# Scale and add in three stretches: the stretches' sizes on a grid of 128 bytes instead of 1 KiB

## The chip, the cores and the metric

One core of a Trainium2 chip. The metric is the device time of one execution in microseconds, the median of several runs. Before the change it is 150.83 us (three runs, 150.75 to 150.89).

## The reference

Two large arrays are read, one is scaled by a single number, and they are added:

```python
B, S, D = 512, 32, 640
x:  (B, S, D) bfloat16
fx: (B, S, D) bfloat16
alpha: (1,) bfloat16

def reference(x, fx, alpha):
    return x + alpha * fx
```

Each array has 10,485,760 elements of 2 bytes, 20.97 MB. Two are read and one is written: 62.9 MB.

## The kernel before

The arrays are taken as one flat row of elements. That row is cut into three stretches by `CUTS`, counted in units of `K` elements a partition: 63, 61 and 36 units of 512 elements (1 KiB). A stretch is a block of consecutive memory, shared out over the 128 partitions of the on-chip memory: partition p has the p-th part of it. In the first stretch each partition's row is 63 KiB long, and the rows of neighbouring partitions begin 63 KiB apart in memory; in the second it is 61, in the third 36.

All data lie in one on-chip tile, `room`, of `ROOM` = 207 units a partition. The arrays do not fit at once, so places in it are used again: a stretch of fx is loaded, scaled in place, added onto x, and its place is free for the next load. A second tile, `kept`, lies in the matmul accumulators' memory (PSUM) and takes 14 units of scaled fx out of `room`, so that a place comes free earlier.

The order is written out by hand in `PLAN`, a line for each step, and `tile_standalone__rezero__sampling_kernel` goes through it:

- `f a b @ t` and `x a b @ t` load the units a to b of fx or x to unit t of `room` (function `transfer`, line 109, all on SyncE's queue).
- `a` loads alpha (line 98), spreads it over the partitions with a matmul by ones (line 103) and copies it to `a_f` (line 104).
- `m t n` scales n units at t by alpha (line 122, VectorE).
- `p t n` copies n scaled units to `kept` (line 127), `q t n` adds `kept` to n units of x (line 139).
- `+ t u n` adds n scaled units at u to n units of x at t (line 144).
- `s a b @ t` stores (line 109); the first store has the words `after + 184`, by which it also waits for the addition at unit 184 (`late`, line 94).

SyncE issues in the order of the plan, and each issue waits until its place in `room` is free, or its data are there. Every issue goes to one queue, which 16 DMA engines work off in order. Each transfer covers all 128 partitions, eight rows for each engine. There are eleven data transfers: the first f load in two parts, the first x load, the second f load, the second x load in two parts, the third f and x loads, three stores.

The rows that a transfer touches are made here:

Of the kernel before, what the change touches and what calls it, by code (L numbers as in the profile page):

```python
# [1 line left out]

# [4 lines left out]

ALU = mybir.AluOpType
F32 = mybir.dt.float32
I32 = mybir.dt.int32  # L10

K = 512
P = 128
ROOM = 207
CUTS = (0, 63, 124, 160)
KEPT = 14

PLAN = """  # L30
f 0 8 @ 144
f 8 63 @ 152
a
x 0 63 @ 0
m 144 63
f 63 124 @ 63
+ 0 144 38
x 63 99 @ 146
+ 38 182 25
x 99 124 @ 182  # L40
m 63 61
p 110 14
f 124 160 @ 110
+ 146 63 36
x 124 160 @ 63
+ 182 99 2
m 110 36
+ 184 101 9
s 0 63 @ 0 after + 184
q 193 14  # L50
s 63 124 @ 146
+ 63 110 36
s 124 160 @ 63
"""


@with_exitstack
def kernel(
    ctx: ExitStack,
    tc: tile.TileContext,  # L60
    x: bass.AP,
    fx: bass.AP,
    alpha: bass.AP,
    out: bass.AP,
):
    nc = tc.nc
    flat = {
        name: t.rearrange("b s d -> (b s d)") for name, t in (("x", x), ("f", fx), ("s", out))
    }
    assert flat["x"].shape[0] == P * CUTS[-1] * K  # L70

    def stretch(what, a, b):
        low, high = next(c for c in zip(CUTS, CUTS[1:]) if c[0] <= a < c[1])
        rows = flat[what][P * low * K : P * high * K].rearrange("(p n) -> p n", p=P)
        return units(rows, a - low, b - low)

    consts = ctx.enter_context(tc.tile_pool(name="consts", bufs=1))
    psum = ctx.enter_context(tc.tile_pool(name="psum", bufs=1, space=bass.MemoryType.PSUM))
    rooms = ctx.enter_context(tc.tile_pool(name="rooms", bufs=1))
    ctx.enter_context(tc.manual_schedule())  # L80

    kept = psum.tile([P, KEPT * K], x.dtype, name="kept")
    room = rooms.tile([P, ROOM * K], x.dtype, name="room")
    a_f = consts.tile([P, 1], F32, name="a_f")
    info = mybir.DependencyInfo(mybir.DependencyClass.Sync, mybir.DependencyReason.DATA)
    done, moved = [], {}

    def units(t, a, b):
        return t[:, a * K : b * K]

    def late(r, after):
        if after:
            what, a = after[1], int(after[2])
            tc.add_manual_dep(r.ins, moved[what, a].ins.name, info, reason="issued late")

    def spread_alpha(after):
        a_1 = consts.tile([1, 1], alpha.dtype, name="a_1")
        done.append(nc.sync.dma_start(out=a_1[:], in_=alpha[None, :]))  # L98
        late(done[-1], after)
        ones = consts.tile([1, P], alpha.dtype, name="ones")  # L100
        nc.vector.memset(ones[:], 1.0)  # L101
        a_ps = psum.tile([P, 1], F32, name="a_ps")
        done.append(nc.tensor.matmul(a_ps[:], ones[:], a_1[:], start=True, stop=True))  # L103
        nc.vector.tensor_copy(out=a_f[:], in_=a_ps[:])  # L104

    def transfer(what, a, b, at, after):
        away, here = stretch(what, a, b), units(room, at, at + b - a)
        out, in_ = (away, here) if what == "s" else (here, away)
        r = nc.sync.dma_start(out=out, in_=in_)  # L109
        late(r, after)  # L110
        moved[what, a] = r
        done.append(r)

    for step in PLAN.strip().split("\n"):
        what, *rest = step.split()
        if what == "a":
            spread_alpha(rest)
        elif what == "m":
            t, n = map(int, rest)
            f = units(room, t, t + n)  # L120
            done.append(
                nc.vector.tensor_scalar(out=f, in0=f, scalar1=a_f[:], scalar2=None, op0=ALU.mult)  # L122
            )
        elif what == "p":
            t, n = map(int, rest)
            done.append(
                nc.vector.tensor_scalar(  # L127
                    out=units(kept, 0, n).bitcast(I32),
                    in0=units(room, t, t + n).bitcast(I32),
                    scalar1=0,  # L130
                    scalar2=None,
                    op0=ALU.bitwise_or,
                )
            )
        elif what == "q":
            t, n = map(int, rest)
            xt = units(room, t, t + n)
            done.append(
                nc.vector.tensor_tensor(out=xt, in0=xt, in1=units(kept, 0, n), op=ALU.add)  # L139
            )  # L140
        elif what == "+":
            t, u, n = map(int, rest)
            xt, f = units(room, t, t + n), units(room, u, u + n)
            moved[what, t] = nc.vector.tensor_tensor(out=xt, in0=xt, in1=f, op=ALU.add)  # L144
            done.append(moved[what, t])
        else:
            a, b, _, at = rest[:4]
            transfer(what, int(a), int(b), int(at), rest[4:])

    last = nc.sync.nop(nofuse=True)  # L150
    for i in done[:-1]:
        tc.add_manual_dep(last.ins, i.ins.name, info, reason="all but the last store")


# [1 line left out]
_INS = ['x', 'fx', 'alpha']  # L156
_OUTS = [((512, 32, 640), 'bfloat16')]


# [23 lines left out]
```

## Time and profile before

| | |
|---|---|
| median of three runs | 150.83 us |
| the profiled execution's own time | 150.75 us |
| its span, first to last instruction | 149.0 us |
| VectorE busy | 69.4 us, 13 instructions |
| DMA queue | 62.92 MB, 422 GB/s over the span |
| read, written | 41.94 MB, 20.97 MB |
| VectorE idle before the first addition, until the first x load | 10.4 us |
| VectorE idle before two scalings, until the second and third f load | 1.4 and 7.0 us |

The span lies inside the device time; 1.75 us of this execution are outside of it. The profile also records every packet that the DMA engines move, with its size, its start and its duration. For data a packet is one partition's row of one transfer, so that each of the 16 engines has 8 packets a transfer and 88 in all.

### The profile page before, as it was taken

The numbers are of one execution on the slowest core, as the hardware profiler recorded it, in microseconds if no ns is written. First come the engines' busy times: TensorE is split into PE (matmuls) and PEld (weight loads), VectorE is DVE, ScalarE is ACT, GpSimd is POOL, SyncE is SP. The second block draws the span as 40 slices with busy tenths as digits, with TensorE's granted clock in tenths as the row PEclk, the third lists the DMA queues.
The fourth block names the chain that finished last, engine by engine and source line by source line (L and its number), as shares of the span: only waits on it lengthen the run. The fifth ranks groups of instructions, "written<-read, shape, count | busy, mean of one in ns | idle before, by whom it ended". The sixth has DMA issues, their size and how long they took to land.

```text
span 149.0 us, 80 instructions
## 1 busy us (share of the span) xinstructions
PE 0.2 (0%) x1; PEld 0.1 (0%) x1; DVE 69.4 (47%) x13; POOL 0.2 (0%) x4
## 2 busy tenths in 40 slices
PE   0000000000000000000000000000000000000000
PEld 0000000000000000000000000000000000000000
DVE  0000009920099996999999009999950000000000
POOL 0000000000000000000000000000000000000000
DMA  5996998996969969989999989999696998969993
GB/s 176 590 439 287 484 519 364 468 537 294 546 268 537 520 285 427 475 376 422 419 454 475 445 346 475 475 436 554 277 554 277 546 419 386 537 268 427 475 475 158
DMA packets 1586, 62.92 MB, mean 422 GB/s; under 512 B 178, under 2 KB 178, under 8 KB 178
## 3 DMA queue, kind: packets, MB, share of 16 engines
q1 hardware_dynamic: 1586, 62.92, 98.0%
HBM read 41.94 MB, written 20.97 MB: 422 GB/s over the span
## 4 chain that ended last, share of the span: by engine, by line
DMA 38%; DVE 27%; DVEq 7%; another core or an unknown queue 1%; SPq 1%; issue 0%
DMA room<-in_x_dram 26%; DVE room L144 13%; DMA room<-in_fx_dram 11%; DVE room L122 9%; DVEq L178 7%; DVE kept L127 3%; DVE room L139 2%; SPq L109 1%; SPq L98 0%; DVEq L122 0%; DVEq L144 0%
## 5 line engine op out<-in xcount | busy, mean ns | idle before, releaser
L144 DVE TENSOR_TENSOR room<-room 128x18432 bf16<-128x18432 bf16 (+4 forms) x6 | 39.7, 6641 | 10.4 <-DMA room<-in_x_dram 10.4
L122 DVE TENSOR_SCALAR room<-room,a_f 128x32256 bf16<-128x32256 bf16 (+2 forms) x3 | 22.0, 7331 | 8.4 <-DMA room<-in_fx_dram 8.3
L104 DVE COPY a_f<-a_ps 128x1 f32<-128x1 f32 x1 | 0.2, 157 | 21.1 <-PE a_ps L103 21.1
L127 DVE TENSOR_SCALAR kept<-room 128x3584 int32<-128x3584 int32 x1 | 3.9, 3894 | 0.0
L139 DVE TENSOR_TENSOR room<-room,kept 128x7168 bf16<-128x7168 bf16 x1 | 3.9, 3881 | 0.0
L101 DVE MEMSET ones<- 1x128 bf16 x1 | 0.2, 165 | 0.8 <-PEq L167 0.8
L103 PE MATMUL a_ps<-a,ones 1*128 1x1 bf16 x1 | 0.2, 158 | 21.9 <-DMA a<-in_alpha_dram 21.9
L167 POOL MEMSET const-uint8-127<- 128x1 uint8 x1 | 0.1, 102 | 0.0
L167 POOL MEMSET const-bfloat16-1.0<- 128x1 bf16 x1 | 0.1, 101 | 0.0
L103 PEld LDWEIGHTS <-ones 1*128 1x128 bf16 x1 | 0.1, 98 | 1.0 <-DVE ones L101 1.0
L167 POOL MEMSET const-float32-0.0<- 128x1 f32 x1 | 0.1, 98 | 0.2 <-issue 0.2
L167 POOL MEMSET const-float32-1.0<- 128x1 f32 x1 | 0.1, 98 | 0.0
## 6 DMA issues: line engine op xcount, KB each, us to landing
room<-in_x_dram SPq DMA_DIRECT2D x2, 4608.0 KB, 18.7
room<-in_x_dram SPq DMA_DIRECT2D x1, 8064.0 KB, 39.1
out_dram<-room SPq DMA_DIRECT2D x1, 8064.0 KB, 22.3
room<-in_fx_dram SPq DMA_DIRECT2D x1, 7808.0 KB, 57.2
out_dram<-room SPq DMA_DIRECT2D x1, 7808.0 KB
room<-in_fx_dram SPq DMA_DIRECT2D x1, 7040.0 KB, 20.9
room<-in_fx_dram SPq DMA_DIRECT2D x1, 4608.0 KB, 17.1
out_dram<-room SPq DMA_DIRECT2D x1, 4608.0 KB, 38.1
```

The source lines that it names most:

```text
L101: nc.vector.memset(ones[:], 1.0)
L103: done.append(nc.tensor.matmul(a_ps[:], ones[:], a_1[:], start=True, stop=True))
L104: nc.vector.tensor_copy(out=a_f[:], in_=a_ps[:])
L109: r = nc.sync.dma_start(out=out, in_=in_)
L122: nc.vector.tensor_scalar(out=f, in0=f, scalar1=a_f[:], scalar2=None, op0=ALU.mult)
L127: nc.vector.tensor_scalar(out=units(kept, 0, n).bitcast(I32), in0=units(room, t, t + n).bitcast(I32), scalar1=0, scalar2=None, op0=ALU.bit ...
L139: nc.vector.tensor_tensor(out=xt, in0=xt, in1=units(kept, 0, n), op=ALU.add)
L144: moved[what, t] = nc.vector.tensor_tensor(out=xt, in0=xt, in1=f, op=ALU.add)
L167: nc = _bacc.Bacc("TRN2", target_bir_lowering=False, num_devices=1)
L178: with _tile.TileContext(nc) as tc:
```

## The change

The unit becomes 64 elements, 128 bytes, an eighth of the one before; `ROOM` and `KEPT` are the same numbers of bytes. The three stretches become 507, 487 and 286 units instead of 504, 488 and 288 such units: rows of 63.375, 60.875 and 35.75 KiB instead of 63, 61 and 36. The plan has the same steps in the same order with the lengths and places that follow. With the new distances between rows, the rows of the partitions begin at more different places modulo 16 KiB of memory; a row's beginning is now a multiple of 128 bytes, and before it was one of 1 KiB.

```diff
-K = 512
+K = 64
 P = 128
-ROOM = 207
-CUTS = (0, 63, 124, 160)
-KEPT = 14
+ROOM = 1656
+CUTS = (0, 507, 994, 1280)
+KEPT = 112
 PLAN = """
-f 0 8 @ 144
-f 8 63 @ 152
+f 0 64 @ 1149
+f 64 507 @ 1213
 a
-x 0 63 @ 0
-m 144 63
-f 63 124 @ 63
-+ 0 144 38
-x 63 99 @ 146
-+ 38 182 25
-x 99 124 @ 182
-m 63 61
-p 110 14
-f 124 160 @ 110
-+ 146 63 36
-x 124 160 @ 63
-+ 182 99 2
-m 110 36
-+ 184 101 9
-s 0 63 @ 0 after + 184
-q 193 14
-s 63 124 @ 146
-+ 63 110 36
-s 124 160 @ 63
+x 0 507 @ 0
+m 1149 507
+f 507 994 @ 507
++ 0 1149 308
+x 507 795 @ 1169
++ 308 1457 199
+x 795 994 @ 1457
+m 507 487
+p 882 112
+f 994 1280 @ 882
++ 1169 507 288
+x 994 1280 @ 507
++ 1457 795 15
+m 882 286
++ 1472 810 72
+s 0 507 @ 0 after + 1472
+q 1544 112
+s 507 994 @ 1169
++ 507 882 286
+s 994 1280 @ 507
 """
```

## The prediction

> **What bounds the kernel now.** I read the page first: busy time, the slices, the DMA queue.
>
> ```profile
> span 149.0 us, 80 instructions
> PE 0.2 (0%) x1; PEld 0.1 (0%) x1; DVE 69.4 (47%) x13; POOL 0.2 (0%) x4
> DMA  5996998996969969989999989999696998969993
> DMA packets 1586, 62.92 MB, mean 422 GB/s; under 512 B 178, under 2 KB 178, under 8 KB 178
> q1 hardware_dynamic: 1586, 62.92, 98.0%
> ```
>
> VectorE, the only engine that computes for long, is busy 47%; the 16 DMA engines are busy 98% of the span. The 178 small packets are completion marks and alpha; the other 1408 are data, 88 on each engine. The trace's records of these packets give the whole time. The first begins 1.74 us into the span, the last ends at 147.84, and the span ends 1.13 us later: 1.74 + 146.10 + 1.13 = 148.97. On each engine one packet follows the other without a gap.
>
> A packet here is one partition's row of one transfer. Medians: 8,192 bytes 309 ns, 25,600 bytes 949, 36,864 bytes 1364 to 1366, 56,320 bytes 2079, 62,464 bytes 2305, 64,512 bytes 2380. From 25,600 to 64,512 bytes that is 1431 ns for 38,912 bytes, 37.7 ns a KiB (27.2 GB/s an engine), and 7 to 8 ns of fixed part. Loads and stores of one size agree within 2 ns. The summed excess over the shortest packet of each size is 0.49 us an engine in the first transfer (8 KiB a row, first rows 307 to 1001 ns), and 0.17 us in all the rest. So the engines are at one rate from 5 us on.
>
> Then the order in time (start, duration, engine, line), cut to SyncE's late issues and VectorE's work ahead of the first store, to see whether a transfer could come late.
>
> ```profile
> 51.57 7.06 SPq L109 DMA_DIRECT2D room<-in_x_dram  x2
> 71.95 0.33 SPq L109 DMA_DIRECT2D room<-in_fx_dram  x1
> 81.60 0.33 SPq L109 DMA_DIRECT2D room<-in_x_dram  x1
> 89.15 5.02 DVE L122 TENSOR_SCALAR room<-room,a_f 128x18432 bf16<-128x18432 bf16 x1 [6.98 <-DMA room<-in_fx_dram]
> 94.09 2.55 DVE L144 TENSOR_TENSOR room<-room 128x4608 bf16<-128x4608 bf16 x1
> 96.56 3.88 DVE L139 TENSOR_TENSOR room<-room,kept 128x7168 bf16<-128x7168 bf16 x1
> 96.67 13.80 SPq L109 DMA_DIRECT2D out_dram<-room  x3
> ```
>
> The tightest place is the first store. It is issued at 96.67, when the addition of 4608 elements ends (94.09 + 2.55). The first engine is through with the last load at 99.03. The kernel's first issue, at 0.73, had its first packet at 1.74, so this store can start at about 97.7 (an estimate from that row): 1.3 us of reserve. The other late issues come over 5 us before the first engine runs dry, with 4 us of reserve by the same estimate (the third f load: issued at 71.95, first engine dry at 77.1).
>
> **The change, part by part.** *Instructions:* the same 13 on VectorE, the same 11 issues on SyncE, each waiting for the same instruction as before; none added, none moved.
>
> *Bytes:* 1280 units of 128 bytes are 160 units of 1 KiB, so the total is unchanged. Rows become 64,896, 62,336 and 36,608 bytes, still one packet each if the limit that I can't see lies above 64,896 (the longest shown is 64,512). 88 packets an engine as before, so the fixed parts are as many: 0.
>
> *VectorE:* the sums of lengths are equal (1168 units of 64 elements added, 146 of 512 before), and 22 + 39.7 us of work moves by 0.14 us at most from one instruction to another (the first addition: 256 elements more, at 10,292 ns / 19,456 each). This hides under the transfers. Without that cover it would cost its 0.14 us.
>
> *When the late issues come:* up to the landing of the third f load, 2274 units are loaded instead of 2272 of equal size: 2 rows' worth of 128 bytes on 8 partitions an engine, 2 x 128 x 8 bytes at 37.7 ns a KiB, 0.08 us later; its multiply is 128 elements shorter (0.03 us at 5021 ns / 18,432). The last load is 2 units shorter, so the end of loading stays. The first store's reserve goes from 1.3 to about 1.2 us: cost 0.
>
> *The start:* what different places can give lies in the first transfer, since only there engines lose time. Its end differs by engine, 2.83 to 3.33 us after the first packet, and the engine that was last there is last at the end (146.10, the first 145.61): nothing later evens it out. If all engines did as well as the best, the gain is 0.49 us; if the new places are worse by as much, the loss is 0.49. Against a large gain: the rows of the third stretch are 36 KiB apart, so that they begin at only four places modulo 16 KiB whatever engine takes which row, and its store ran at 1364.0 ns for all 128 rows; at the borders between stretches, where the pattern of places changes, no packet is longer either. So the place alone doesn't slow an engine in the full stream, and the slow rows may as well be the cold start of 16 streams. I take -0.1 us.
>
> *Rows off their boundaries:* before, all rows in memory begin at multiples of 1 KiB. Now the odd partitions of the first and second stretch begin 128 bytes past a multiple of 256. Each engine meets such rows in 8 of the 11 transfers (three of f, three of x, two stores; all but the three of the last stretch); four rows each if odd partitions spread evenly, 32 of 88. No row here shows what one costs. Lower bound 0: on the on-chip side the rows are off already (the room begins at byte 16,832 of a partition in the built program, 192 past a multiple of 256), and loads that write there and stores that read there run alike, 2380 ns for 64,512 bytes both ways. Upper bound, one more small packet a row: the 4-byte packets take 9 ns, 32 x 9 = 0.29 us. I take 0.1, nearer the lower end, as the on-chip rows are the nearer kin.
>
> [...]
>
> **Sum** against the profiled execution's own 150.75 us: -0.1 + 0.1 = 0, so 150.75; its median of three is 0.08 higher, so 150.8 as the forecast.
>
> **Rivals.** *Faster: the start was a collision of places and is gone.* For it: the excess sits in the first rows of engines that begin together (300 to 700 ns), and is gone once they have drifted some 0.5 us, about 14 KB, apart. Against it: the third stretch, above. With the whole spread gone, -0.49 us, and with the off rows free: 150.3; with their upper price 150.6. It is more than 0.2% (0.30 us, about what a measurement of this kernel can tell from no change) from 0.3 of the 0.49 on. [...]
>
> *Slower: rows that begin off the boundary run at a lower rate, not just with a late start.* The place is the 32 off rows of each engine, 4 x (309 + 2079 + 2380 + 2305 + 1364 + 949 + 2380 + 2305) = 56.3 us of its 146. [...] It decides from 0.5% on (0.30 us). For it: both sides being off by different amounts, and stores that share 256 bytes between two rows, are new, and nothing hides a DMA rate at 98% busy. Against it: a row's on-chip side was off by 192 bytes against its memory side all along, at full rate. The late first store is no rival of weight: it needs another 1.2 us of delay, and the sizes give 0.1.
>
> *The change doesn't reach what it says:* 286 units are 35.75 KiB, so the third stretch still has few places; that gives the forecast's time and is part of its chance.
>
> **How the numbers follow.** Forecast (both terms small): 0.38, between 150.5 and 151.1. Faster by the start: 0.28, 150.2 to 150.5. Slower by the off rows: 0.34; two thirds of it between 151.1 and 152.3, a third above. It gets much although the nearest rows speak against it, since that price has no row at all and no upper end. So faster 0.28, within 0.2% 0.38, slower 0.34. Range 150.3 to 152.3: it leaves out some 0.07 below and 0.11 above. The forecast's own range is 150.5 to 151.1.
>
> **What would show it.** Each step: the first transfer's end by engine (2.83 to 3.33 us after the first packet; below 2.9 on all of them for the collision); the medians by row size against 37.7 ns a KiB and 8 ns (64,896 bytes: 2394 ns; 62,336: 2300; 36,608: 1355; more on odd partitions of two stretches for the off rows, and none in the last stretch); the share of the queue, 98%, and the first store issued near 96.7 with no gap behind the last load. The prediction is wrong if the medians lie over 1% above these, if rows are cut into more than 88 packets an engine, or if the spread of the start shrinks by over 0.3 us.

## The result, and the profile after

The changed kernel takes 151.27 us (median of 7, 151.12 to 151.46) against 150.83 (median of 7, 150.71 to 150.90): a ratio of 1.003, 95% interval 1.0018 to 1.0041. It is slower by 0.44 us. The forecast was 150.8, no change; the range, 150.3 to 152.3, holds the time.

The page of the changed kernel, the lines that answer to those shown of before:

```profile
span 149.4 us, 80 instructions
PE 0.2 (0%) x1; PEld 0.1 (0%) x1; DVE 69.4 (46%) x13; POOL 0.2 (0%) x4
DMA  5988996969899699799999799999796969969993
DMA packets 1586, 62.92 MB, mean 421 GB/s; under 512 B 178, under 2 KB 178, under 8 KB 178
q1 hardware_dynamic: 1586, 62.92, 97.9%
```

As many packets, as many bytes, the same work on VectorE, and a queue that is as full. The profiled execution took 151.18 us, 0.43 more than that of before. The packets begin at 1.74 us and end at 148.21: 1.74 + 146.47 + 1.19 = 149.40. So 0.37 of the 0.43 lie between the first packet and the last, the rest behind the last.

The order in time of the changed kernel (start, duration, engine, line):

```profile
52.27 7.03 SPq L110 DMA_DIRECT2D room<-in_x_dram  x2
...
72.44 0.33 SPq L110 DMA_DIRECT2D room<-in_fx_dram  x1
82.09 0.33 SPq L110 DMA_DIRECT2D room<-in_x_dram  x1
89.52 4.99 DVE L123 TENSOR_SCALAR room<-room,a_f 128x18304 bf16<-128x18304 bf16 x1 [6.88 <-DMA room<-in_fx_dram]
94.42 2.55 DVE L145 TENSOR_TENSOR room<-room 128x4608 bf16<-128x4608 bf16 x1
96.89 3.88 DVE L140 TENSOR_TENSOR room<-room,kept 128x7168 bf16<-128x7168 bf16 x1
97.00 13.73 SPq L110 DMA_DIRECT2D out_dram<-room  x3
```

Everything here is 0.3 to 0.7 us later, and none of it made itself late: each step follows the loads (the 0.7 at 52.27 has in it 0.13 of the first addition, which is 256 elements longer). The first store is issued at 97.00, and the first engine is through with the last load at 99.52, so there is no gap. The lateness is there much earlier. The waits of the matmul that spreads alpha, first before, then after; alpha lies in the queue behind the first f load:

```profile
PE a_ps L103 <- DMA a<-in_alpha_dram: 21.9, 1, 21.9
```

```profile
PE a_ps L104 <- DMA a<-in_alpha_dram: 22.4, 1, 22.4
```

The exact starts are 21.87 and 22.39. Alpha is one packet of 2 bytes, so this is the lateness of the one engine that moves it; the means over the engines come below. Three more units on eight rows explain 0.11 us (3 x 8 x 128 bytes at 36.8 ns per 1000); 0.41 are lost. The first addition waits for the first x load, before, then after:

```profile
41.25 17.03 DVE L144 TENSOR_TENSOR room<-room 128x19456 bf16<-128x19456 bf16 x2 [10.37 <-DMA room<-in_x_dram]
```

```profile
41.82 17.13 DVE L145 TENSOR_TENSOR room<-room 128x19712 bf16<-128x19712 bf16 x2 [10.37 <-DMA room<-in_x_dram]
```

The same reckoning gives 0.34 lost here (six units more), 0.32 at the second scaling (59.64 and 60.15, five), 0.29 at the third (89.15 and 89.52, two). So the loss comes about in the first loads, and then stays.

The packet records show what kind of loss it is. The medians are those of before on the same line: 64,896 bytes 2394 ns, 62,336 bytes 2300, 36,608 bytes 1354. No row is slower as a rule. But single rows are: in the first f load 15 of 128 rows took over 20 ns more than the median (up to 267 ns), in the first x load 16 (up to 111), in the second f load 9; before, none in any of the three. For the experiments I use one measure that holds longer rows and gaps between rows: the *step*, from the start of a row to the start of the next on its engine, less its bytes at 36.76 ns per 1000 (27.2 GB/s). An undisturbed step is about 5 ns: the medians by transfer in the kernel before are 4.7 to 5.8, and 7.9 in the third f and the last x load. Means in ns a row, over the engines whose rows can be followed through the records (14 to 16 of them):

```
                 first f, 8 KiB   first f, rest   first x   second f   last x   stores
before                66               5.8          6.5        7.6      16.1   6.2 5.5 4.7
after                 74              31.2         34.1       14.2       7.7   5.6 5.7 4.9
```

Times eight rows, the differences are 0.07, 0.20, 0.22, 0.05 and -0.07 us. One profile stands behind each line: the kernel with the early store, below, loads the same bytes to the same places as the kernel before up to its last load, and its start took 86, so the 0.07 is within what the start does by itself.

### The profile page after: what moved, and what is told of

Its sections match the earlier page's. It is cut to its first block, busy times and chain, and to the rows that moved or that the text cites. A ratio compares the mean times of both kernels' runs of the same rounds, so it can differ in the third digit from the quotient of the medians.

```text
span 149.4 us, 80 instructions
## 1 busy us (share of the span) xinstructions
PE 0.2 (0%) x1; PEld 0.1 (0%) x1; DVE 69.4 (46%) x13; POOL 0.2 (0%) x4
## 3 DMA queue, kind: packets, MB, share of 16 engines
q1 hardware_dynamic: 1586, 62.92, 97.9%
## 4 chain that ended last, share of the span: by engine, by line
DMA 38%; DVE 27%; DVEq 7%; another core or an unknown queue 1%; SPq 1%; issue 0%
DMA room<-in_x_dram 27%; DVE room L145 13%; DMA room<-in_fx_dram 11%; DVE room L123 9%; DVEq L179 7%; DVE kept L128 3%; DVE room L140 2%; SPq L110 1%; SPq L99 0%; DVEq L123 0%; DVEq L145 0%
## 5 line engine op out<-in xcount | busy, mean ns | idle before, releaser
L145 DVE TENSOR_TENSOR room<-room 128x19712 bf16<-128x19712 bf16 (+5 forms) x6 | 39.7, 6640 | 10.4 <-DMA room<-in_x_dram 10.4
L123 DVE TENSOR_SCALAR room<-room,a_f 128x32448 bf16<-128x32448 bf16 (+2 forms) x3 | 22.0, 7331 | 8.1 <-DMA room<-in_fx_dram 8.1
```

## The experiments

Three theories at first. 1: rows that begin 128 bytes past a multiple of 256 are delayed when they are loaded. 2: the distance between rows makes engines collide. 3: only the first transfer, the start, falls out another way. The plan keeps its steps and their order, with the lengths and places that follow from the stretches; the diffs show the stretches. Each kernel was timed beside the kernel before (150.85 to 150.94 us). Where units at the end are left out, three transfers are shorter, by 0.11 us a unit in all (3 x 8 x 128 bytes at 36.8 ns per 1000). Where an early expectation says 0.08 or 0.04, it counted one transfer, and 0.23 and 0.11 are right; the later ones say 0.12.

**Off the 1 KiB grid, on the 256-byte grid**

```diff
-CUTS = (0, 507, 994, 1280)
+CUTS = (0, 506, 992, 1280)
```

> Stretches of 506, 486 and 288 units of 128 bytes: the two large stretches leave the grid of 1 KiB, but every row still begins at a multiple of 256 bytes. Theory 1, rows that begin 128 bytes past a multiple of 256 are delayed while they are loaded: none here, so 150.8 us, and rows loaded between 10 and 60 us of the span exceed the shortest of their size by under 0.05 us an engine in sum (0.03 before, 0.18 in the changed kernel). Theory 2, the new distances between rows bring the engines into each other's way: as in the changed kernel, 151.1 to 151.4 us, and an excess of 0.1 to 0.2 us in that stretch. Theory 3, only the first transfer falls out another way: excess as before, and the time follows the engine that ends the first transfer last.

151.06 us, ratio 1.0009 (1.0000 to 1.0018). Steps 6.4 in the first f, 6.8 in the first x, 7.6 in the second f load: undisturbed. What it may lose lies in the start (93 ns a row; the last engine ends the first transfer 3.71 us after the first packet, 3.33 before), and the old distances gave up to 86 there. This distance, off the grid of 1 KiB, disturbed nothing in the stream.

**All rows off the boundary, old distances**

```diff
-CUTS = (0, 504, 992, 1280)
+CUTS = (0, 504, 992, 1278)
-rows = flat[what][P * low * K : P * high * K]
+rows = flat[what][SHIFT + P * low * K : SHIFT + P * high * K]
```

SHIFT is 64 elements (128 bytes) here.

> The distances between rows of before (504 and 488 units), with the arrays begun 128 bytes later in memory, so that every row begins 128 bytes past a multiple of 256. The last stretch has 286 units; the first 128 bytes of the output and its last 32 KB are left out, which takes 0.08 us off. Theory 1: 88 off rows an engine in place of 32, so 151.2 us or more (the changed kernel's loss of 0.4 to 0.5 at least), with scattered longer rows in all loads, the last stretch's too. Theory 2: 150.75 us and no longer rows behind the start. Theory 3: 150.75 give or take 0.3, the excess behind the start as before.

150.84 us, ratio 0.9999 (0.9990 to 1.0008).

**The same with 256 bytes**

> As the one with the arrays begun 128 bytes later, but 256 bytes later: the same places to each other, every row at a multiple of 256 bytes; the first 256 bytes of the output and its last 32 KB are left out. Theories 1 and 2: 150.75 us and no longer rows behind the start. If it is as slow as the one with 128 bytes, it is leaving the grid of 1 KiB, or the left-out edges, that count and not the boundary of 256.

150.67 us, ratio 0.9986 (0.9977 to 0.9995): the 0.23 us that are left out, so no loss. The pair shows the price of off rows: 0.17 us for all 88 of an engine, against 32 in the changed kernel. Off loads have the medians of aligned ones (within 2 ns) and, in the first two, their steps (first f 5.9 and 5.8, first x 6.8 and 6.7, for 128 and 256 bytes). In the second f and the last x load four rows each took 20 to 150 ns more with 128 bytes and none with 256; that is some 0.04 us in all. The stores differ (9.2, 11.2, 10.3 against 6.2, 5.5, 4.7), 4.8 ns a row in the mean, 0.11 us over 24 rows. Theory 1, which was about loads and needed ten times as much, falls. And in the changed kernel the stores' steps are those of before: its off rows cost nothing there that shows. Half of its rows in two stores begin off the boundary, so beginning off alone is not shown to cost the 4.8 ns; with all rows off, each row ends off as well.

**The on-chip places 128 bytes later**

```diff
-return t[:, a * K : b * K]
+o = OFF if t is room else 0
+return t[:, o + a * K : o + b * K]
```

OFF is 64 elements, and the tile is longer by as much.

> The kernel before with the room's places 128 bytes later on chip (at byte 64 past a multiple of 256 where they were at 192), memory untouched. The changed kernel does this to most of its places. Theories 1 and 2: 150.8 us, no change. If the on-chip side has the price, 151.1 us or more, and longer rows in all transfers, stores among them.

150.94 us, ratio 1.0003 (0.9994 to 1.0012), steps as before. The on-chip places show no price.

**The changed kernel again**

> The changed kernel once more, to see what of its profile is its own and what is chance. If the longer rows between 10 and 60 us (0.18 us an engine in sum) belong to the kernel, they are there again within a factor of two, and the time is 151.2 to 151.3 us; if they were chance, under 0.05 us, and the time nears 150.9.

151.35 us, ratio 1.0037 (1.0024 to 1.0049). First x 27.4 ns a row again, and 16 rows over 20 ns; but the first f load has 11.2 (14.9 over all 16 engines) and the second f 6.9, and the start took more (89). The disturbance belongs to the kernel; its share by transfer changes from run to run.

**One place for all engines**

```diff
-CUTS = (0, 507, 994, 1280)
+CUTS = (0, 480, 960, 1280)
```

Stretches of 480, 480 and 320 units, rows of 60, 60 and 40 KiB.

> [...] The idea behind the change, fewer places mean more collisions: the first transfer's excess grows far beyond 0.5 us an engine, and the time above 151.3 us. Theory 2 in its narrow form, only rows at odd multiples of 128 bytes disturb the stream: no longer rows behind the start, and the time is that of before, 150.8 to 150.9, give or take what the start gives.

151.61 us, ratio 1.0050 (1.0037 to 1.0064), and yet the start is usual (83 ns a row) and the first loads undisturbed (5.6, 6.3, 7.9). The loss is in one place that nobody expected: the last x load, 100 ns a row. Its first store was issued at 94.81, 1.9 us earlier than before. The later pair on the first store takes this up. One place is also a supposition: rows 60 KiB apart begin at four places modulo 16 KiB (63 KiB apart, at sixteen), and the records don't say which engine takes which row.

**The odd distance in one stretch alone**

```diff
+CUTS = (0, 507, 995, 1279)
```

> 507, 488 and 284 units: only the first stretch has the odd distance (the last 16 KB of the output are left out, 0.04 us). If the odd distance disturbs the stream where it is used, longer rows up to 40 us of the span (some 0.12 us an engine in sum), none after, and 151.0 us. If it takes both stretches, or the change of distance at 41 us, none.

```diff
+CUTS = (0, 504, 991, 1279)
```

> 504, 487 and 288 units: only the second stretch has the odd distance (the last 16 KB of the output are left out, 0.04 us). Where the odd distance disturbs the stream: longer rows from 40 to 80 us alone, some 0.1 us an engine, start as before, and 150.9 us. If the harm comes from the first transfer alone, as before: 150.8.

507 in the first stretch: 151.21, ratio 1.0024 (1.0015 to 1.0033); with the 0.11 us left out, this is the whole loss of the change. 487 in the second: 150.83, ratio 0.9997 (0.9988 to 1.0005). Where the first x load landed, by the timeline (first addition, with 507, then with 487):

```profile
41.91 17.13 DVE L133 TENSOR_TENSOR room<-room 128x19648 bf16<-128x19648 bf16 x2 [10.39 <-DMA room<-in_x_dram]
```

```profile
41.38 17.03 DVE L133 TENSOR_TENSOR room<-room 128x19520 bf16<-128x19520 bf16 x2 [10.14 <-DMA room<-in_x_dram]
```

0.53 us apart, 0.23 of it from six more units. Steps of the first x load 28.9 against 7.4; of the second f load 7.0 against 7.8. So 487, odd too, is harmless there, and the question is now which distances harm.

**Other sizes of the first stretch.** Theory A: odd multiples of 128 bytes. The second stretch is 488 in each; the third takes what is left, of 1279 units with an odd first stretch and 1280 with an even one.

```diff
+CUTS = (0, 505, 993, 1279)
+CUTS = (0, 509, 997, 1279)
+CUTS = (0, 487, 975, 1279)
+CUTS = (0, 508, 996, 1280)
```

> 505, 488 and 286 units: another odd distance in the first stretch, the rest even (the last 16 KB of the output are left out, which over three transfers takes 0.12 us off; the 0.04 us told of the kernels with 507, 488 and 284 and with 504, 487 and 288 counted one transfer, and the 0.08 of those begun 128 and 256 bytes later should be 0.23). Theory A, an odd multiple of 128 bytes between rows makes engines collide in the first loads: rows of the first stretch's x load take 20 ns or more a row over 36.8 ns per 1000 bytes in the mean (7 before, 27 to 34 with 507), while their median stays at 5, and 151.1 us. Theory B, it is something of 507 alone: 7 ns, and 150.75 to 150.9.

> 509, 488 and 282 units, a third odd distance in the first stretch (the last 16 KB of the output are left out, 0.12 us). Theory A: as with 505, 20 ns or more a row in the first x load, 151.1 us. Theory B: 7 ns, and 150.75 to 150.9.

> 487, 488 and 304 units: the odd distance that did no harm in the second stretch, now in the first (the last 16 KB of the output are left out, 0.12 us). Theory A with the addition that the engines must run abreast as at the start: 20 ns or more a row in the first x load. If 487 is harmless as such: 7 ns. The time is less telling, as the last load and the first store stand otherwise to each other: 151.1 or more against 150.9.

> 508, 488 and 284 units: the first stretch on a grid of 512 bytes, whole output. Theory A: no odd distance, 7 ns a row in the first x load, 150.8 to 151.0, the start deciding within this. If every distance off the grid of 1 KiB does harm: 20 ns or more and 151.2.

Then, from what these gave, 497 and 511, and 510 between two odd ones:

```diff
+CUTS = (0, 497, 985, 1279)
+CUTS = (0, 511, 999, 1279)
+CUTS = (0, 510, 998, 1280)
```

> 497, 488 and 294 units (the last 16 KB of the output are left out, 0.12 us): an odd distance between 487 and 505. Theory A with nearness, odd distances harm the more the nearer rows come to 64 KiB apart: 7 to 15 ns a row in the first x load (7 with even distances, 18 with 505). If 487 is the exception and every other odd distance harms: 20 or more. Time 150.8 to 151.0.

> 511, 488 and 280 units (the last 16 KB of the output are left out, 0.12 us): rows 128 bytes short of 64 KiB. With nearness: 30 ns or more a row in the first f and x loads, and 151.4 us or more. If nearness is not it: 18 or less.

> 510, 488 and 282 units, whole output: an even distance between 509 and 511, 256 bytes short of 64 KiB. If nearness to 64 KiB alone does the harm: a start or first loads between those of 509 and 511, and 151.4 us or more. If it takes an odd multiple of 128 bytes too: 7 ns a row in the first x load, the start as usual (65 to 90 ns a row), and 150.9.

By first stretch; the start is the first 8 KiB of each row, steps in ns a row, "long" the rows of the first x load that took over 20 ns more than their median; all 128 rows are counted. 506 is the first experiment, 507 the kernel with 507 in one stretch alone; there is one profile of each:

```
units  short of 64 KiB  start  first f  first x  long   ratio to before (95%)
504        1024 B         66      5.8      6.5     0    (the kernel before)
506         768 B         93      6.4      6.8     0    1.0009 (1.0000 to 1.0018)
508         512 B         87      6.2      6.9     0    0.9998 (0.9989 to 1.0007)
510         256 B         76      6.6      6.3     0    1.0003 (0.9994 to 1.0012)
487        3200 B         85      6.2      6.0     0    1.0039 (1.0027 to 1.0052)
497        1920 B         84      6.4     10.9     0    1.0012 (1.0001 to 1.0023)
505         896 B         85      6.7     18.0     6    1.0010 (1.0001 to 1.0018)
507         640 B        101     11.4     28.9    19    1.0024 (1.0015 to 1.0033)
509         384 B         80     26.7     32.5    13    1.0037 (1.0024 to 1.0051)
511         128 B        211     31.6      5.4     0    1.0087 (1.0074 to 1.0100)
```

The kernels with an odd number do 0.11 us less work than the others, so that some 0.0007 is to be added to their ratios. Even distances were undisturbed, down to 256 bytes short of 64 KiB (first f 5.8 to 6.6, first x 6.3 to 6.9). Odd ones grew worse the nearer they came to it, by the steps of the start and both loads taken together, from 497 (84, 6.4 and 10.9) to 511 (211, 31.6 and 5.4). The times alone don't part 497 from 505, and 507 and 509 lie as close as two profiles of one kernel (first f 31.2 and 11.2 in the changed kernel). It is the distance and not the length of a row: the first f load is cut into rows of 8 KiB and some 55 KiB, and its rows were long too from 507 to 511. Nor is it the place on chip: the first x load goes to the beginning of `room` in all of them. 487 has no long row, and its ratio comes from the last load (87 ns a row, the early store below). I had expected theory A's 20 ns at 505 and got 18, and for 511 30 ns or more in the x load: there the loss came earlier, in the first f load. Its start took 211 ns a row, so that the second transfer's first rows began 4.32 us after the first packet in the mean (3.08 before), and the first x load ran free. Its page and wait for alpha:

```profile
span 150.4 us, 80 instructions
...
q1 hardware_dynamic: 1586, 62.87, 97.2%
```

```profile
PE a_ps L92 <- DMA a<-in_alpha_dram: 23.6, 1, 23.6
```

Alpha comes 1.7 us later than before, of which seven more units are 0.26. Its queue's share of 97.2% is the lowest of all.

**The early first store.** The one-place kernel with its first store held back:

```diff
-s 0 480 @ 0 after + 1511
-q 1544 112
+q 1544 56 0
+s 0 480 @ 0 after q 1544
+q 1600 56 56
```

The step `q` has a third number here, the place in `kept` from which it adds.

> The kernel with 480, 480 and 320 units (one place), its first store held back until half of the addition of the kept units is done, so that it is issued near 96.7 us of the span and not at 94.8. If that kernel's loss was the store queued too early behind the last load, the last load's excess falls from 0.75 to under 0.1 us an engine and the time to 150.9 to 151.0; then one place modulo 16 KiB costs nothing. If the one place was the loss: still 151.5 or more.

And the kernel before, its plan written in units of 64 elements, with its store made early:

```diff
-+ 1456 792 16
++ 1456 792 60
-+ 1472 808 72
-s 0 504 @ 0 after + 1472
++ 1516 852 28
+s 0 504 @ 0 after + 1516
```

> The kernel before with 60 in place of 16 units added ahead of the last scaling, so that the first store is issued about 1.5 us earlier, near 95.1. Nothing else is changed. If a store that is queued early slows the last load, its excess rises from under 0.1 to some 0.65 us an engine, and the time to 151.4 or 151.5. If the long rows belonged to rows of 38 and 40 KiB: 150.85.

The timeline of the one-place kernel, then held back, then the kernel before as it was (its store was issued at 96.67), then with the early store:

```profile
94.81 17.36 SPq L98 DMA_DIRECT2D out_dram<-room  x3
100.98 10.83 DVE L133 TENSOR_TENSOR room<-room 128x20480 bf16<-128x20480 bf16 x1 [2.40 <-DMA room<-in_x_dram]
```

```profile
96.82 2.27 SPq L99 DMA_DIRECT2D out_dram<-room  x2
100.28 10.82 DVE L135 TENSOR_TENSOR room<-room 128x20480 bf16<-128x20480 bf16 x1 [1.55 <-DMA room<-in_x_dram]
```

```profile
100.35 9.75 DVE L144 TENSOR_TENSOR room<-room 128x18432 bf16<-128x18432 bf16 x1
```

```profile
95.19 15.88 SPq L98 DMA_DIRECT2D out_dram<-room  x3
100.95 9.76 DVE L133 TENSOR_TENSOR room<-room 128x18432 bf16<-128x18432 bf16 x1 [1.99 <-DMA room<-in_x_dram]
```

The last addition starts when the last x load has landed, and it lands later where the store was issued earlier. Held back, the one-place kernel takes 150.96, ratio 1.0006 (0.9997 to 1.0014); the early store makes the kernel before take 151.54, ratio 1.0045 (1.0033 to 1.0057). So the one-place kernel's four places modulo 16 KiB, or one if the supposition holds, cost nothing that can be measured, and the store queued 1.5 us earlier cost 0.65 us. The addition of the kept units starts together with the store in the two slow ones; held back, the store goes alone, the addition still starts at 94.78, and the load is not slowed. So it is the store.

## Why the prediction was wrong

*The bound* was right: the 16 DMA engines, 98.0% busy before and 97.9% after. The end moved by what the loads lost, and nothing else in the kernel moved of itself.

*Bytes, VectorE, late issues:* right. 88 rows an engine, one packet each up to 65,408 bytes; medians as forecast (2394 and 2300 ns, 1354 for 1355); no gap at the first store.

*The start: -0.1 us.* No gain came: the first transfer's steps went from 66 to 74 ns a row in the first profile, 89 in the second (+0.07 and +0.19 us). A loss isn't shown either: in the one-place kernel they were 83, and with four kernels on the old distances of the first stretch 72 to 86 (on-chip places moved, arrays 256 bytes later, 487 in the second, the early store). The start isn't seen to follow the number of places; my doubt that it does was right, and yet I kept a tenth for it. The rival that the start was a collision of places falls with the same runs.

*The step that failed* stands in the same part: "what different places can give lies in the first transfer, since only there engines lose time", and "So the place alone doesn't slow an engine in the full stream". I took both from the kernel before, and the second from its third stretch, whose rows are 36 KiB apart. For places modulo 16 KiB it holds as far as it was tried: the one-place kernel's first loads ran free (5.6, 6.3 and 7.9 ns a row). But I read it as if no distance could slow the stream, and so the sum has no term for the loads behind the first transfer. They lost 0.48 us in the mean of the engines (0.20, 0.22 and 0.05 in the rest of the first f, the first x and the second f load). The distance of the first stretch's rows was enough for it: 507 there alone lost as much. The third stretch couldn't speak for 507: its distance is even and far from 64 KiB.

*Rows off their boundaries: +0.1 us.* The size was near what it costs when all rows are off (0.17), but it isn't what the changed kernel is seen to pay: its loads' medians and its stores' steps are unmoved. Loads with all rows off have the medians of aligned ones within 2 ns; stores with all rows off paid 4.8 ns a row in the mean.

*The rival that forecast slower* had the right side and the wrong mechanism. It asked for a lower rate on off rows, so for moved medians; 0.44 us would have been 0.8% there. What happened is scattered long rows: a tenth of those in three loads long by 20 to 270 ns, the others at full rate. What I named as signs (medians by size) would have cleared it, and did. So the range holds the time by luck: its upper part was there for a cost that didn't come. And none of the three signs of being wrong came up (medians, number of packets, spread of the start, 0.49 and now 0.55 us), since none of them sees single long rows behind the start.

*Distances near 64 KiB:* the trace of before ran free at 36 KiB (1364 ns a row of the last store). In the runs, nearness to 64 KiB did matter, but only with odd multiples of 128 bytes (ratio 1.0087 at 128 bytes short of it); 256 and 512 bytes short of it were as good as 1024 (1.0003 and 0.9998). No run here has a distance of 64 KiB itself, or one above it.

*Open:* why it takes an odd multiple. Two things go with it and these runs don't part them: neighbouring rows lie alternately on and off the 256-byte boundary, and rows four apart differ by an odd multiple of 512 bytes. Both go with 487 too, which has no long row, so nearness to 64 KiB is needed as well. That loads with all rows off lost some 0.04 us in all speaks against off rows as such, not against the alternation. Open too is why the first store, with rows of the same length and distance as the first x load, has no long row (5.6 ns a row): it is a store, and it comes later. How far apart the engines run doesn't settle it. In the kernel before their rows start 0.50 us apart at the first x load and 0.48 at the third store; at the first x load they start 0.69 us apart both in the changed kernel's second profile, with 16 long rows, and in that of 511, with none.

## What to carry to other kernels

When a kernel keeps the DMA engines busy throughout (98% of the span here), ask for each transfer what the distance between its rows is; here clean rows 36 KiB apart said nothing of rows 63.375 KiB apart. Row distances that were multiples of 256 bytes left the first loads undisturbed at every size tried (first x load 6.3 to 6.9 ns a row), and odd multiples of 128 bytes near 64 KiB cost up to 1.3 us (511 units: 152.23 us against 150.89). The median row hid such a loss (2394 ns in the changed kernel's first x load, as forecast): compare the mean of the step with its median, transfer by transfer (34.1 and 7.4 ns there, 6.5 and 5.5 before).

## What was not expected of the hardware

A store queued early behind the last load slowed that load. In three kernels the first store was issued 3.6 to 5.1 us before the first engine ended the last load, and the last load's rows lost 0.64 to 0.77 us an engine over the shortest row of the size; with 1.9 to 2.5 us it lost under 0.09 (0.08 in the kernel before, with seven long rows). The long rows all began before any row of the store did: in the one-place kernel the last rows of the load, begun from 97.89 to 98.44 us, took 1936 to 2238 ns where 1514 is usual, and the store's first row began at 99.91. So it is not the traffic of the store's rows, as the records have them, that was in the way; what it is, no run here shows. The kernel before holds its first store back by the words `after + 184`. No run here drops them; a store 1.5 us earlier cost 0.65 us.
